# Attention plus two-layer feed-forward on one core: GpSimd's arithmetic moved to VectorE, and a new order by hand

## The chip, the core and the metric

The kernel runs on one core of a Trainium2 chip. The metric is the device time of one launch in microseconds (us). The core has five engines that run their own instruction streams and meet at semaphores: TensorE (PE in the rows; its weight loads are listed apart as PEld), VectorE (DVE), ScalarE (ACT), GpSimd (POOL) and SyncE (SP, which here only issues DMAs). Matmuls read SBUF and write PSUM; VectorE and ScalarE read both. GpSimd's queue also issues the DMAs that add to or convert what they move.

## What is computed

```python
# q, k, v: 2 x 6016 x 256; w_in: 256 x 2048; w_out: 2048 x 256; alpha: 2048
qn = q / (np.linalg.norm(q, axis=1, keepdims=True) + 1e-06)
kn = k / (np.linalg.norm(k, axis=1, keepdims=True) + 1e-06)
s = kn.transpose(0, 2, 1) @ qn / tau          # 256 x 256 for each batch
a = softmax(s)                                # over the last axis
x = (v @ a).reshape(12032, 256)
h = x @ w_in
g = np.maximum(h, 0.0) + alpha * np.minimum(h, 0.0)
return g @ w_out
```

## The kernel before

The softmax matrix of a batch is folded into the first weight: M = a @ w_in is made once for each batch, so that the first layer is one product of v and M. Every float32 operand of a matmul is split into a high part and a remainder of a shorter float type, and one product is three matmuls (`passes`: high by high, high by low, low by high).

The 12032 rows are 24 tiles of 500 to 504 (12 for each batch), and a tile is 8 **items**, one for each pair of 128-wide blocks of the 2048 hidden columns: 192 items, numbered i = 8 * tile + pair. The first layer of every item is a seven-product scheme in place of eight (`pe_a`, `pe_b`, `pe_c`, `pe_d`: 21 matmuls of 250 columns into PSUM tiles q and r). ScalarE copies q to r and p (`copies`), VectorE adds p (`add_p7`), ScalarE multiplies by alpha (`act_n`) and VectorE takes the maximum (`dve_g`), which gives g.

The second layer has two forms. In the plain form g is split (`g_high` on ScalarE, `g_low` on VectorE) and multiplied in 12 matmuls of 500 columns (`n_half`, 6 in `s2_first` and 6 in `s2_second`). In the **S form** (`is_s`) it too is a seven-product scheme, 21 matmuls of 250 columns. It needs sums of the weights, made once for each pair (`s_weights`), and sums of g (`g_sums` on VectorE, tile t), whose remainder is made by negating the high part on ScalarE (`t_low`, tile tgl) and by a DMA that adds t to it (the **adding DMA**, issued by GpSimd in `t_low`). `s2_first` holds 9 matmuls that need g alone (tiles xh, xl); `s2_second` holds the 12 that need tgh and tgl. S items are the pairs 0, 2, 4, 6 in batch 0 and 0, 1, 2, 4, 5, 6 in batch 1, in the tiles of `S_TILES`.

The sign of alpha - 1 decides between maximum and minimum; it is folded into the weights of w_out. To pay for that, h has to be multiplied by the sign. In batch 0 that is done in the maximum (a scalar_tensor_tensor with `sgn`). In batch 1 the w_in that M is made from was multiplied by it beforehand: `reload_wi` brings a part of w_in and the row of alpha back, `sign_wi` makes the sign and multiplies on GpSimd, then `split_wi_h` (ScalarE) and `split_wi_l` (VectorE) split it for `m1_pe`.

GpSimd also makes the weight sums: `s_weights` (five additions and subtractions for each of six pairs) and one subtraction in `s_weights_split`.

What sets the order: all steps from the first item on are put in one list. `put(i, at, f, ...)` gives a step the place 5.0 * i + at + MOVED, the list is sorted, and each engine runs its instructions in that order. `MOVED` is a table of shifts, one dictionary for each item of a named stretch: "first" (from item 0), "early" (which repeats for every tile), "soft" and "m1" (where the softmax and M of batch 1 are made beside the tiles of batch 0), "late" (repeats for the tiles of batch 1), "last". gh and gl (and tgh and tgl, which share their buffers) have 3 buffers each, raw (xh, xl, weight sums, w_in parts) has 4, r's first tile has 2.

Of the kernel before, what the change touches and what calls it, by code (L numbers as in the profile page):

```python
# [14 lines left out]
P = 128  # L15
# [8 lines left out]
SIDE = 3.7  # L24
# [32 lines left out]
W_ITEMS = (3, 100, 4, 6, 102, 7)  # L57
# [10 lines left out]
CHAIN = dict(sums=(2, 4.0), norms=(3, 2.0), norms2=(3, 4.0), bcast=(4, 3.7), score0=(5, 3.7),  # L68
             score1=(6, 2.0), exp0=(6, 3.7), exp1=(7, 1.7), pt=(8, 3.7), eT0=(8, 4.0), eT1=(8, 6.0))
MOVED = {  # L70
    ("first", 0): dict(add_p70=2.65, copies=-1.66, keep_wi=-4.85, pe_a=-1.98, pe_b=-1.87,
# [4 lines left out]
    ("first", 2): dict(act_n0=0.29, act_n1=0.15, add_p70=0.83, add_p71=-0.13, copies=-1.01,
        dve_g0=0.68, dve_g1=2.22, g_high0=1.69, g_high1=-0.3, g_low0=2.77, g_low1=2.8,
        pe_a=-2.34, pe_b=-2.28, pe_c=-0.67, pe_d=-2.39, pe_s2=-1.85, wo_next=0.31),
    ("first", 3): dict(act_n0=-0.49, act_n1=-0.77, add_p70=0.2, add_p71=-0.41, copies=-0.8,
# [12 lines left out]
    ("first", 6): dict(act_n0=-0.93, act_n1=0.03, add_p70=-0.17, add_p71=0.8, copies=-0.41,
        dve_g0=-0.35, dve_g1=1.1, g_high0=1.19, g_high1=0.05, g_low0=4.11, g_low1=3.63,
        pe_a=-1.39, pe_b=-0.56, pe_c=-0.53, pe_d=-1.51, pe_s2=-1.44, s_weights=5.59,
        s_weights_split=-3.34, v_low0=-1.85),
    ("first", 7): dict(act_n0=0.17, act_n1=1.1, add_p70=-0.01, add_p71=0.12, copies=0.98,
        dve_g0=0.1, dve_g1=1.34, g_high0=3.72, g_high1=0.43, g_low0=3.86, g_low1=2.9, pe_a=-3.35,
        pe_b=-0.47, pe_c=0.2, pe_d=-2.03, pe_s2=-1.18, s_weights=0.6, v_low1=-1.55, v_low2=-3.0),
    ("first", 8): dict(act_n0=-0.92, act_n1=1.3, add_p70=-0.46, add_p71=1.24, copies=-1.37,
        dve_g0=-0.32, dve_g1=0.29, evac=0.27, g_high0=-1.28, g_high1=1.67, g_low0=0.53,  # L100
        g_low1=-0.19, pe_a=-2.86, pe_b=-1.76, pe_c=-0.65, pe_d=0.4, pe_s2=-0.9,
        s_weights_split=-0.43, v_sums0=-5.6),
    ("first", 9): dict(act_n0=-1.29, act_n1=0.41, add_p70=1.14, add_p71=0.09, copies=0.95,
# [1432 lines left out]
```

## Time and profile before

| | |
|---|---|
| three timed runs | 1137.88, 1143.43 and 2400.7 us |
| their median | 1143.43 us |
| the profiled execution, its own time | 1135.38 us |
| span of its instructions | 1133.6 us |
| granted TensorE clock | 1.0 of full speed throughout |

Stages by the time in the span: 0 to 100 us products of k and q and M of batch 0; about 100 to 145 tile 0; 145 to 190 tile 1; 190 to 430 the other S tiles of batch 0; 430 to 560 the softmax of batch 1 beside tiles of batch 0; 560 to 690 M of batch 1; 690 to 1080 the S tiles of batch 1; 1080 to the end the last tile. A matmul's end is modelled in these profiles and overlaps the next one, so the idle time that PE shows is somewhat less than what a stall costs, and the idle time of PEld somewhat more.

### The profile page before, as it was taken

Reading aid. Unit: us, or ns where it says so; the run is one execution under the profiler, and the core shown is the slowest. Engines: PE = TensorE matmul, PEld = TensorE weight load, DVE = VectorE, ACT = ScalarE, POOL = GpSimd, SP = SyncE. Lnnn points to the kernel's source line nnn. Section 1 sums busy time; section 2 is a strip of 40 time slices with the busy share of each in tenths; the row PEclk is TensorE's granted clock in tenths of the full one; section 3 lists DMA queues with packets and bytes.
Section 4 is the critical chain, followed back from the end, with each engine's and each line's share of the span. In section 5 each row is a group of like instructions: output and inputs, shape, how many; then the busy total and the mean of one; then the engine's idle time right before and its main releaser. Section 6 shows DMA issues by size and latency. Waiting matters only on the chain.

```text
span 1133.6 us, 20976 instructions
## 1 busy us (share of the span) xinstructions
PE 1103.0 (97%) x7788; PEld 1028.4 (91%) x7788; DVE 971.4 (86%) x1830; ACT 911.4 (80%) x1556; POOL 193.6 (17%) x220
## 2 busy tenths in 40 slices
PE   9999999999999999999999999999999999999998
PEld 8888788999999899999988889999999999999997
DVE  6798987998898898878889878998898898898974
ACT  6798687888888888678767768888888888889874
POOL 0001521011011011011244411211211121111100
PEclk9999999999999999999999999999999999999999
DMA  9997334654654554034421216556656756656620
GB/s 333 364 324 258 93 97 104 148 126 94 147 128 108 135 122 108 19 91 90 103 68 58 70 33 133 128 107 133 134 110 123 145 109 123 133 121 124 120 55 19
DMA packets 70389, 142.81 MB, mean 126 GB/s; under 512 B 6416, under 2 KB 38416, under 8 KB 70160
## 3 DMA queue, kind: packets, MB, share of 16 engines
q0 software_dynamic: 31616, 66.22, 31.9%
q1 hardware_dynamic: 38672, 75.26, 19.5%
q8 instruction: 62, 1.02, 0.4%
q14 instruction: 39, 0.32, 0.1%
HBM read 60.83 MB, written 14.42 MB: 66 GB/s over the span
## 4 chain that ended last, share of the span: by engine, by line
PE 35%; DMA 9%; DVE 5%; ACT 4%; issue 3%; POOL 0%; ACTq 0%; POOLq 0%; DVEq 0%
DMA tgl<-t 9%; PE X L441 6%; PE X L442 6%; PE X L440 5%; PE r L440 4%; PE r L442 4%; PE r L441 4%; PE o L1214 2%; ACT g L993 2%; PE q L442 1%; PE q L441 1%; PE q L440 1%; ACT tgl L1094 1%; DVE gl L1018 1%; DVE r L980 1%
## 5 line engine op out<-in xcount | busy, mean ns | idle before, releaser
L440 PE MATMUL r<-vs,m 128*128 128x250 f32 (+1 forms) x960 | 273.8, 285 | 8.6 <-DVE r L980 7.0
L442 PE MATMUL r<-vs,m 128*128 128x250 f32 (+1 forms) x960 | 268.2, 279 | 0.0
L441 PE MATMUL r<-vs,m 128*128 128x250 f32 (+1 forms) x960 | 268.2, 279 | 0.0
L980 DVE TENSOR_TENSOR r<-r,p 128x250 f32<-128x250 f32 (+1 forms) x384 | 162.5, 423 | 62.9 <-PE r L442 50.4
L440 PEld LDWEIGHTS r<-vs,m 128*128 128x128 f32 x960 | 180.8, 188 | 22.7 <-DVE r L980 10.4
L1095 POOL DMA_DIRECT2D tgl<-t x96 | 83.2, 866 | 608.9 <-ACT tgl L1094 580.1
L441 PEld LDWEIGHTS r<-vs,m 128*128 128x128 f32 x960 | 181.1, 189 | 5.2
L993 ACT ACTIVATE g<-r,alpha_sb 128x500 f32<-128x500 f32 (+1 forms) x192 | 131.2, 686 | 63.8 <-DVE r L980 42.1
L442 PEld LDWEIGHTS r<-vs,m 128*128 128x128 f32 x960 | 181.5, 189 | 0.0
L993 ACT ACTIVATE g<-r,salpha 128x500 f32<-128x500 f32 (+1 forms) x192 | 130.2, 682 | 54.1 <-DVE r L980 29.4
L1003 DVE TENSOR_TENSOR g<-r,g 128x500 f32<-128x500 f32 (+1 forms) x192 | 128.0, 675 | 35.8 <-ACT g L993 34.3
L1005 DVE SCALAR_TENSOR_TENSOR g<-r,sgn,g 128x500 f32<-128x500 f32 (+1 forms) x192 | 140.6, 733 | 18.2 <-ACT g L993 18.0
L1018 DVE TENSOR_TENSOR gl<-g,gh 128x500 fp32r<-128x500 f32 (+1 forms) x192 | 135.5, 711 | 8.8 <-ACT gh L1014 7.6
L963 ACT COPY r<-q 128x500 f32<-128x500 f32 (+1 forms) x192 | 110.1, 573 | 32.7 <-DVE g L1005 14.0
L1014 ACT CAST gh<-g 128x500 fp32r<-128x500 f32 (+1 forms) x192 | 116.5, 615 | 21.2 <-DVE g L1005 11.5
L441 PE MATMUL X<-gl,wo 128*128 128x500 f32 (+1 forms) x320 | 125.1, 391 | 1.4 <-DVE gl L1018 1.4
L440 PE MATMUL X<-gh,wo 128*128 128x500 f32 (+1 forms) x320 | 125.3, 391 | 0.0
L442 PE MATMUL X<-gh,wo 128*128 128x500 f32 (+1 forms) x320 | 124.9, 390 | 0.0
L440 PE MATMUL q<-vs,m 128*128 128x250 f32 (+1 forms) x384 | 107.9, 281 | 0.0
L442 PE MATMUL q<-vs,m 128*128 128x250 f32 (+1 forms) x384 | 107.2, 279 | 0.0
L441 PE MATMUL q<-vs,m 128*128 128x250 f32 (+1 forms) x384 | 107.2, 279 | 0.0
L1094 ACT ACTIVATE tgl<-t 128x1000 fp32r<-128x1000 f32 (+1 forms) x96 | 99.8, 1040 | 1.8 <-DVE t L1072 1.0
(152 smaller groups left out, 2733.7 us busy)
## 6 DMA issues: line engine op xcount, KB each, us to landing
tgl<-t POOLq DMA_DIRECT2D x66, 500.0 KB, 4.6
tgl<-t POOLq DMA_DIRECT2D x30, 504.0 KB, 4.7
kqT<-kqT_dram SPq DMA_DIRECT2D x20, 512.0 KB, 3.6
kq<-k_dram SPq DMA_DIRECT2D x39, 256.0 KB, 5.4
kq<-q_dram SPq DMA_DIRECT2D x39, 256.0 KB, 5.4
v<-vT_dram SPq DMA_DIRECT2D x16, 500.0 KB, 5.4
vs<-vt POOLq DMA_DIRECT2D x32, 250.0 KB, 4.8
outT_dram<-c SPq DMA_DIRECT2D x30, 250.0 KB, 2.6
```

The costliest lines, as they stand in the source:

```text
L440: nc.tensor.matmul(out, wh, xh, start=first, stop=False, **s)
L441: nc.tensor.matmul(out, wh, xl, start=False, stop=False, **s)
L442: nc.tensor.matmul(out, wl, xh, start=False, stop=last, **s)
L963: nc.scalar.copy(r_t[i][0][:, :, :h], x[:, 0:1, :h].broadcast_to([P, 2, h]))
L980: nc.vector.tensor_tensor(out=r[1][:, n, :h], in0=r[0][:, 1, :h], in1=p7_t[i][:, :h], op=ALU.add)
L993: nc.scalar.activation(blocks(g_t[i], i, 2 * fi, 2 * fi + 2), r_t[i][fi][:, :, : half_of(i)], AF.Copy, scale=(alpha_sb if tiles[items[i][0 ...
L1003: nc.vector.tensor_tensor(out=g, in0=r_t[i][fi][:, :, : half_of(i)], in1=g, op=ALU.max)
L1005: nc.vector.scalar_tensor_tensor(out=g, in0=r_t[i][fi][:, :, : half_of(i)], scalar=sgn[:, f : f + 1], in1=g, op0=ALU.mult, op1=ALU.max,)
L1014: nc.scalar.copy(gs_t[i][0][:, fi, :w], g_t[i][:, fi * w : fi * w + w])
L1018: nc.vector.tensor_tensor(out=gs_t[i][1][:, fi, :w], in0=g_t[i][:, fi * w : fi * w + w], in1=f32(gs_t[i][0][:, fi, :w]), op=ALU.subtract,)
L1094: nc.scalar.activation(ts_t[i][1][:, :w], tt_t[i][:, :w], AF.Copy, scale=-1.0)
L1095: nc.gpsimd.dma_start(out=ts_t[i][1][:, :w], in_=tt_t[i][:, :w], accum_op=ALU.add)
```

## The change

Nothing that is computed changes, but for the place of the sign of batch 1. Six things:

1. `sign_wi` and the row of alpha are gone. `reload_wi` loads the part of w_in alone, and batch 1 uses the same scalar_tensor_tensor with `sgn` in `dve_g`, and `salpha` in `act_n`, as batch 0.
2. `s_weights` and its subtraction run on VectorE, each of the five operations as a step of its own. Their items (`W_ITEMS`) go from 3, 100, 4, 6, 102, 7 to 9, 67, 10, 11, 69, 13.
3. Tile 1 is no longer an S tile, and "early" begins one tile later.
4. Steps that held several instructions are cut in single ones that can be placed apart: `wo_next` (into `split_wo`, `conv_a`, `conv_b`), `m_sums` (into `m_scaled` and four), `m_split`, `combine`, `norms2`.
5. GpSimd keeps only memory fills at the start and DMA issues.
6. The whole of `MOVED` is new.

```diff
-W_ITEMS = (3, 100, 4, 6, 102, 7)
+W_ITEMS = (9, 67, 10, 11, 69, 13)
...
-        pe_b=0.05, pe_c=0.17, pe_d=-0.31, s2_first=-0.82, s2_second=-2.41, t_high=-2.16,
...
+        s2_first=-0.07, s2_second=-0.67, t_high=0.84, t_low=0.18, v_low0=-0.46, x_high=-0.65,
...
     def reload_wi(j):
-        x = raw.tile([P, KC + 1, 256], F32, tag="raw", name=f"wi{j}")
-        nc.sync.dma_start(out=x[:, :KC], in_=wi_kept[:, j])
-        row = alpha_row[j * 256 : j * 256 + 256]
-        nc.sync.dma_start(out=x[:, KC], in_=row.partition_broadcast(P))
-        wi_raw[j] = x
-
-    def sign_wi(j):
-        w, x = wi_raw[j][:, :KC], wi_raw[j][:, KC]
-        nc.gpsimd.tensor_scalar(out=x, in0=x, scalar1=1.0, scalar2=-2.0, op0=ALU.is_gt, op1=ALU.mult)
-        nc.gpsimd.tensor_scalar(out=x, in0=x, scalar1=1.0, scalar2=None, op0=ALU.add)
-        x = wi_raw[j][:, KC : KC + 1].broadcast_to([P, KC, 256])
-        nc.gpsimd.tensor_tensor(out=w, in0=w, in1=x, op=ALU.mult)
+        wi_raw[j] = raw.tile([P, KC, 256], F32, tag="raw", name=f"wi{j}")
+        nc.sync.dma_start(out=wi_raw[j], in_=wi_kept[:, j])
...
-            scale=(alpha_sb if tiles[items[i][0]][0] else salpha)[:, f : f + 1],
+            scale=salpha[:, f : f + 1],
...
-        if tiles[items[i][0]][0]:
-            nc.vector.tensor_tensor(out=g, in0=r_t[i][fi][:, :, : half_of(i)], in1=g, op=ALU.max)
-            return
...
-    S_TILES = [t for t in range(1, len(tiles) - 1) if t not in (per_b - 4, per_b - 1, per_b)]
+    S_TILES = [t for t in range(1, len(tiles) - 1) if t not in (1, per_b - 4, per_b - 1, per_b)]
...
+    def s_weights(n, k):
+
+        if k == 0:
+            sw_t[n] = raw.tile([P, 8, P], F32, tag="raw", name=f"sw{n}")
+        x = sw_t[n]
+        fs = slice(2 * S_J[n], 2 * S_J[n] + 2)
+        a = [f32(wo[:, l, fs]).rearrange("p f m -> p (f m)") for l in range(2)]
+        o, i0, i1, op = (
+            (x[:, 0:4].rearrange("p b m -> p (b m)"), a[0], a[1], ALU.add),
+            (x[:, 4], x[:, 1], x[:, 3], ALU.add),
+            (x[:, 5], x[:, 4], x[:, 0], ALU.subtract),
+            (x[:, 6], x[:, 1], x[:, 0], ALU.subtract),
+            (x[:, 7], x[:, 2], x[:, 5], ALU.subtract),
+        )[k]
+        nc.vector.tensor_tensor(out=o, in0=i0, in1=i1, op=op)
...
-        nc.gpsimd.tensor_tensor(out=ws[0][:, n, 1], in0=x[:, 4:8], in1=f32(ws[0][:, n, 0]), op=ALU.subtract)
+    def s_weights_low(n):
+        x = sw_t[n]
+        nc.vector.tensor_tensor(out=ws[0][:, n, 1], in0=x[:, 4:8], in1=f32(ws[0][:, n, 0]), op=ALU.subtract)
...
-            ("first", 0), ("early", NPAIR + 5), ("soft", soft + 2), ("early", soft + 2 * NPAIR),
+            ("first", 0), ("early", 2 * NPAIR + 5), ("soft", soft + 2), ("early", soft + 2 * NPAIR),
```

The two lines of `MOVED` above belong to pair 4 of a tile in "late". What they and their neighbours do to the instructions is seen in the order of each engine.

TensorE, tile 17 (batch 1), item 140 (pair 4), just ahead of the matmuls that need its adding DMA. Before:

```order
L440 MATMUL X2_17_9988<-xh140_10136,wo_114 128x250
L441 MATMUL X2_17_9988<-xl140_10137,wo_114 128x250
L442 MATMUL X2_17_9988<-xh140_10136,wo_114 128x250
L440 MATMUL r0_143_10203<-vs17_9179,m1_7_7501 128x250
L441 MATMUL r0_143_10203<-vs17_9179,m1_7_7501 128x250
L442 MATMUL r0_143_10203<-vs17_9179,m1_7_7501 128x250
L440 MATMUL X3_17_9981<-tgh140_10180,ws_1130 128x250
L441 MATMUL X3_17_9981<-tgl140_10181,ws_1130 128x250
```

And now:

```order
L486 MATMUL r0_144_10190<-vs18_9620,m1_0_6778 128x250
L487 MATMUL r0_144_10190<-vs18_9620,m1_0_6778 128x250
L488 MATMUL r0_144_10190<-vs18_9620,m1_0_6778 128x250
L486 MATMUL q145_10211<-vs18_9620,m1_1_6854 128x250
L487 MATMUL q145_10211<-vs18_9620,m1_1_6854 128x250
L488 MATMUL q145_10211<-vs18_9620,m1_1_6854 128x250
L486 MATMUL q145_10211<-vs18_9620,m1_1_6854 128x250
L487 MATMUL q145_10211<-vs18_9620,m1_1_6854 128x250
L488 MATMUL q145_10211<-vs18_9620,m1_1_6854 128x250
L486 MATMUL X3_17_9914<-tgh140_10094,ws_1472 128x250
L487 MATMUL X3_17_9914<-tgl140_10095,ws_1472 128x250
```

The matmul that reads tgl140 stood behind the first layer of item 143; it now stands behind first-layer work of items 144 and 145. From the last matmul of r of item 140 to the first that reads tgh140 or tgl140 there were 90 matmuls, and there are 120.

ScalarE, the same item, from its first multiplication by alpha to the negation that the adding DMA follows. Before:

```order
L993 ACTIVATE g140_10107<-r1_140_10025,alpha_sb_119 128x500
L700 ACTIVATE vs18_9720<-vs18_9720 128x4x250
L993 ACTIVATE g140_10107<-r0_140_10024,alpha_sb_119 128x500
L1014 CAST gh139_10093<-g139_10029 128x500
L1077 CAST xh140_10136<-g140_10107 128x750
L963 COPY r0_142_10159<-q142_10121 128x2x250
L964 COPY p7_142_10161<-q142_10121 128x250
L993 ACTIVATE g141_10164<-r1_141_10088,alpha_sb_119 128x500
L993 ACTIVATE g141_10164<-r0_141_10087,alpha_sb_119 128x500
L1094 ACTIVATE tgl140_10181<-t140_10169 128x1000
```

And now:

```order
L1045 ACTIVATE g140_10005<-r1_140_9904,salpha_111 128x500
L1154 CAST tgh138_9939<-t138_9895 128x1000
L1045 ACTIVATE g140_10005<-r0_140_9903,salpha_111 128x500
L736 ACTIVATE vs18_9620<-vs18_9620 128x4x250
L1045 ACTIVATE g141_10041<-r1_141_9981,salpha_111 128x500
L1015 COPY r0_142_10043<-q142_10028 128x2x250
L1016 COPY p7_142_10045<-q142_10028 128x250
L1131 CAST xh140_10075<-g140_10005 128x750
L1045 ACTIVATE g141_10041<-r0_141_9980,salpha_111 128x500
L1148 ACTIVATE tgl140_10095<-t140_10048 128x1000
```

The number of instructions up to the negation is the same; a cast of item 138 (tgh138) has come in and a cast of item 139 (gh139) has gone ahead of them, and the high part xh140 is cast later.

VectorE in tile 1, from the first addition to r of item 9 to the first to r of item 10 (vt2 is the sums of v for tile 2). Before:

```order
L980 TENSOR_TENSOR r1_9_1399<-r0_9_1398,p7_9_1400 128x252
L1072 TENSOR_TENSOR t8_1429<-g8_1396 128x504
L1072 TENSOR_TENSOR t8_1429<-g8_1396,t8_1429 128x252
L980 TENSOR_TENSOR r1_9_1399<-r0_9_1398,p7_9_1400 128x252
L1072 TENSOR_TENSOR t8_1429<-g8_1396,t8_1429 128x252
L1005 SCALAR_TENSOR_TENSOR g9_1454<-r1_9_1399,sgn_110,g9_1454 128x504
L980 TENSOR_TENSOR r1_10_1450<-r0_10_1449,p7_10_1451 128x252
```

And now, from the second addition to r of item 9:

```order
L1032 TENSOR_TENSOR r1_9_1373<-r0_9_1372,p7_9_1374 128x252
L1103 TENSOR_TENSOR sw2_1309<-sw2_1309 128x128
L1103 TENSOR_TENSOR sw3_1436<-wo_114 128x512
L701 TENSOR_TENSOR vt2_1364<-v2_1222,vt2_1364 128x252 x2
L1103 TENSOR_TENSOR sw2_1309<-sw2_1309 128x128
L1054 SCALAR_TENSOR_TENSOR g9_1438<-r1_9_1373,sgn_110,g9_1438 128x504
L1103 TENSOR_TENSOR sw0_1244<-sw0_1244 128x128
L1032 TENSOR_TENSOR r1_10_1419<-r0_10_1418,p7_10_1420 128x252
```

The sums t8 of the S form are gone from tile 1, and four operations of the weight sums (sw0, sw2, sw3) stand in the same place, between two additions that TensorE needs.

## Rows read from the trace of the kernel before

**Rows 1.** The page's first part: each engine's busy us, share of the span, instructions.

```profile
PE 1103.0 (97%) x7788; PEld 1028.4 (91%) x7788; DVE 971.4 (86%) x1830; ACT 911.4 (80%) x1556; POOL 193.6 (17%) x220
```

**Rows 2.** Busy time by stage: stretch, its length, then each engine's busy us (instructions).

```profile
100.00:145.00 45.00, 42.47 (x261) 37.10 (x259) 41.31 (x66) 34.93 (x68) 17.71 (x21) 1.00 0.31 102
145.00:190.00 45.00, 41.98 (x294) 38.83 (x295) 36.67 (x70) 35.83 (x64) 6.21 (x7) 1.00 0.45 110
430.00:560.00 130.00, 128.99 (x907) 119.97 (x906) 111.49 (x224) 99.49 (x179) 11.42 (x14) 1.00 0.32 75
560.00:690.00 130.00, 122.59 (x819) 110.69 (x818) 110.67 (x202) 91.78 (x173) 48.20 (x46) 1.00 0.25 66
690.00:1080.00 390.00, 381.32 (x2971) 365.07 (x2970) 344.76 (x664) 336.33 (x542) 74.35 (x84) 1.00 0.62 124
```

**Rows 3.** Waits of the whole span: engine, line, releaser: total us, times, longest us.

```profile
PEld X L441 <- DMA tgl<-t: 19.1, 33, 2.4
PE X L441 <- DMA tgl<-t: 11.9, 21, 2.2
```

**Rows 4.** Waits from 100 to 145 us, TensorE's for VectorE's remainder of g.

```profile
PEld o L1214 <- DVE gl L1018: 3.8, 4, 2.0
PE o L1214 <- DVE gl L1018: 2.5, 2, 1.7
```

**Rows 5.** Waits from 560 to 690 us, TensorE's for VectorE's addition to r.

```profile
PEld r L440 <- DVE r L980: 7.9, 8, 2.9
PE r L440 <- DVE r L980: 5.4, 5, 2.5
```

**Rows 6.** Time line of PE: start, us, engine, line, operation, tiles, columns.

```profile
442.67 0.28 PE L442 MATMUL X<-tgh,ws 128*128 128x250 f32 x1
442.79 0.28 PE L440 MATMUL X<-tgh,ws 128*128 128x250 f32 x1
...
444.90 0.39 PE L440 MATMUL X<-gh,wo 128*128 128x500 f32 x1
445.12 0.39 PE L441 MATMUL X<-gl,wo 128*128 128x500 f32 x1
```

**Rows 7.** Tile tgl: from the adding DMA's issue to its landing.

```profile
DMA to landing us min/median/max: 4.5/4.6/7.0
```

**Rows 8.** Time line of PE in tile 1: a matmul that waited for the adding DMA.

```profile
172.38 0.39 PE L441 MATMUL X<-tgl,ws 128*128 128x252 f32 x1 [2.17 <-DMA tgl<-t]
```

**Rows 9.** Time line of GpSimd and VectorE in tile 0: two remainders of g.

```profile
131.82 1.26 POOL L1048 TENSOR_TENSOR sw<-wo 128x512 f32<-128x512 f32 x1
...
130.09 4.40 DVE L1018 TENSOR_TENSOR gl<-g,gh 128x504 fp32r<-128x504 f32 x2
```

**Rows 10.** Time line of GpSimd, ScalarE, TensorE and VectorE around 585 us.

```profile
583.25 1.08 POOL L603 TENSOR_SCALAR wi<-wi 128x256 f32<-128x256 f32 x1 [10.62 <-DMA wi<-alphar_dram]
...
585.36 1.34 POOL L606 TENSOR_TENSOR wi<-wi 128x512 f32<-128x512 f32 x1
...
590.13 0.62 ACT L610 CAST wis<-wi 128x512 fp32r<-128x512 f32 x1 [3.46 <-POOL wi L606]
...
585.27 2.30 DVE L924 TENSOR_TENSOR mx<-mx 128x128 f32<-128x128 f32 x4
```

**Rows 11.** Time line of VectorE: the same four subtractions 21 us later.

```profile
606.91 1.34 DVE L924 TENSOR_TENSOR mx<-mx 128x128 f32<-128x128 f32 x4
```

**Rows 12.** VectorE's groups by line and shape, 560 to 690 us: busy, mean ns.

```profile
L1018 DVE TENSOR_TENSOR gl<-g,gh 128x500 fp32r<-128x500 f32 x18 | 13.3, 748 | 0.8 <-ACT gh L1014 0.8
```

**Rows 13.** The same, 690 to 1080 us.

```profile
L1018 DVE TENSOR_TENSOR gl<-g,gh 128x500 fp32r<-128x500 f32 x26 | 17.5, 672 | 2.0 <-ACT gh L1014 2.0
```

**Rows 14.** The whole span by line: the maximum with and without sign, another subtraction.

```profile
L1005 DVE SCALAR_TENSOR_TENSOR g<-r,sgn,g 128x500 f32<-128x500 f32 (+1 forms) x192 | 140.6, 733 | 18.2 <-ACT g L993 18.0
L1003 DVE TENSOR_TENSOR g<-r,g 128x500 f32<-128x500 f32 (+1 forms) x192 | 128.0, 675 | 35.8 <-ACT g L993 34.3
...
L614 DVE TENSOR_TENSOR wis<-wi,wis 128x512 fp32r<-128x512 f32 x8 | 5.4, 681 | 0.0
```

More of the change, by code (lines that the diff above doesn't have):

```diff
@@ new lines @@
+    ("first", 13): dict(act_n0=-1.38, act_n1=1.88, add_p70=-0.35, add_p71=-0.23, copies=-0.06,
+        dve_g0=0.09, dve_g1=1.3, g_high0=1.21, g_high1=5.18, g_low0=1.36, g_low1=3.22,
+        load_T0=-5.71, load_T1=0.38, load_T2=-0.28, pe_a=-1.22, pe_b=-2.38, pe_c=-0.58,
+        pe_d=-0.28, s2_first=-1.58, s2_second=-1.28, s_weights0=-8.01, s_weights1=-3.93,
+        s_weights2=-0.2, s_weights3=-4.13, s_weights4=1.96, s_weights_low=5.55, square_T0=-8.35,
+        square_T1=-1.31, square_T2=-3.73, v_low1=-0.18),
@@ new lines @@
+    ("first", 14): dict(act_n0=1.19, act_n1=-0.13, add_p70=1.23, add_p71=-0.24, copies=-0.44,
+        dve_g0=1.12, dve_g1=-0.23, g_high0=-0.37, g_high1=1.27, g_low0=-0.64, g_low1=3.83,
+        pe_a=-2.88, pe_b=1.28, pe_c=-2.02, pe_d=1.51, s2_first=-2.94, s2_second=-2.55,
+        s_weights_high=6.88, v_low2=-2.58),
+    ("first", 15): dict(act_n0=0.28, act_n1=1.12, add_p70=-0.85, add_p71=0.85, copies=1.64,
+        dve_g0=0.99, dve_g1=0.78, g_high0=5.63, g_high1=-0.33, g_low0=4.6, g_low1=0.78,
+        pe_a=0.02, pe_b=-0.39, pe_c=0.41, pe_d=-0.13, s2_first=1.98, s2_second=0.97,
+        s_weights_low=-0.68),
@@ new lines @@
+    ("first", 16): dict(act_n0=-1.92, add_p70=-2.3, add_p71=-0.55, copies=0.52, dve_g0=0.17,
+        dve_g1=-0.94, g_high0=0.6, g_high1=-1.57, g_low0=0.86, g_low1=-1.46, pe_a=-1.34,
+        pe_b=-1.8, pe_c=-1.23, pe_d=-1.68, s2_first=-0.34, s2_second=-1.53, v_sums0=-1.63),
+    ("first", 17): dict(act_n0=-1.45, act_n1=-1.08, add_p70=2.23, add_p71=-1.43, copies=-0.56,
+        dve_g0=-1.19, dve_g1=0.44, g_high0=3.0, g_high1=3.25, g_low0=4.69, g_low1=3.65,
+        pe_a=-1.49, pe_b=1.42, pe_c=-1.92, pe_d=-0.56, s2_first=1.84, s2_second=0.6,
+        v_high1=2.75, v_high2=3.78, v_sums1=-2.16),
@@ new lines @@
+    ("late", 7): dict(act_n0=0.29, act_n1=1.85, add_p70=0.74, add_p71=-2.26, copies=-0.16,
+        dve_g0=0.29, dve_g1=1.77, g_sums0=2.41, g_sums1=2.4, g_sums2=0.86, pe_a=-3.02,
+        pe_b=-0.05, pe_c=-2.97, pe_d=-1.09, s2_first=-2.59, s2_second=0.73, t_high=-1.68,
+        t_low=2.11, x_high=1.28, x_low=0.57),
+    ("last", 0): dict(act_n0=1.06, act_n1=2.64, add_p70=1.01, add_p71=1.41, copies=-2.62,
+        dve_g0=1.12, dve_g1=2.71, g_high0=-2.17, g_high1=1.86, g_low0=3.13, g_low1=3.33,
+        pe_a=-3.8, pe_b=-0.7, pe_c=0.39, pe_d=-0.18, pe_s2=-0.8),
@@ L333 @@
+    ("last", 6): dict(pe_s2=17.95),
 }
@@ L908, in m_pe, with m_scaled @@
                     )
-    def m_sums(at, j):
+    def m_scaled(at, j):
         b = at.b
@@ L1322, in fused_kernel @@
                 nxt += 1
-            m_sums(a0, j)
+            m_scaled(a0, j)
+            for n in range(4):
+                m_sums(a0, j, n)
             if j:
@@ L1418, in fused_kernel @@
                 put(i, TILE["copy"], combine_copy, t)
-                put(i, TILE["sums"], combine, t)
+                for n in range(3):
+                    put(i, TILE["sums"], combine, t, n)
             put(i + 1, TILE["out0"], finish_out, t, 0)
```

636 lines of the change are left out of this document (332 added, 304 removed).

## The prediction

> **What bounds it now.** I read the page's first part, then the stages, then who waited. TensorE is busy for 1103.0 of 1133.6 us and VectorE for 971.4 [rows 1]. The stage of 430 to 560 us shows what TensorE looks like when nothing is late: 128.99 of 130 us [rows 2]. So the kernel is bound by TensorE's own work, and only what TensorE waits for can be won: 30.6 us by its idle time. The loss lies in four stages [rows 2]: 2.5 us in 100 to 145, 3.0 in 145 to 190, 7.4 in 560 to 690 and 8.7 in 690 to 1080. A matmul of 250 columns follows the one before it after 0.12 us though it is shown as 0.28 long [rows 6], so each stall costs up to 0.16 us more than the idle time shows. The idle time of the weight loads counts the same stall from the load, and is my upper bound for each kind of stall; that of the matmuls is the lower.
>
> Two kinds of stall hold most of it. The first is the adding DMA: matmuls waited for tgl for 11.9 us by their own idle time (21 stalls) and 19.1 by that of the loads (33) [rows 3]. It lands 4.5 to 7.0 us after its issue [rows 7]; the worst wait, 2.17 us, is in tile 1 [rows 8], the others are spread over all S tiles, most of them under 1 us. The second is VectorE being late in the two stages where GpSimd computes: for the remainder of g in tile 0, 2.5 to 3.8 us [rows 4], and for the addition to r while M of batch 1 is made, 5.4 to 7.9 us [rows 5].
>
> **Why VectorE is late there.** Two remainders of g took 4.40 us while GpSimd computed beside them [rows 9]; at the 672 ns that one takes in batch 1 [rows 13] they would take 1.35. Four subtractions of 128 columns took 2.30 us beside GpSimd's product and 1.34 alone [rows 10, 11]. The remainder of g takes 748 ns on the mean where GpSimd computes for a third of the time, and 672 where GpSimd only issues DMAs, though it does that for 74 of 390 us [rows 2, 12, 13]. So GpSimd's arithmetic slows VectorE's operations on two SBUF tensors, and its DMA issues do not. Beside that, one stall was a plain chain: the alpha row's DMA held GpSimd for 10.62 us, GpSimd held ScalarE's cast of w_in for 3.46 [rows 10], and everything behind that cast came late.
>
> **The change, part by part.**
>
> *TensorE's work.* Tile 1 turns four S items into plain ones: 12 matmuls of 500 columns at 0.229 us for 21 of 250 at 0.117 (the start-to-start distances of [rows 6], with neighbours): 2.75 for 2.46, so 4 x 0.29 = **+1.2 us**. TensorE's order has 36 matmuls fewer, which agrees. VectorE and ScalarE lose the work of the S form there; I do not count that, since it is not what is waited for.
>
> *The adding DMA.* In the new order the matmuls that read tgl stand later. Counted over the 60 S items of batch 1, at 0.117 and 0.229 us for each matmul, the way from the last matmul of r to the first that reads tgh or tgl grows from 12.3 to 13.7 us on the mean and from 11.5 to 12.6 at the least; in batch 0 from 12.7 to 14.1. Item 140, shown above, grows from 11.9 to 15.4. On ScalarE the work from an item's alpha to the negation is about as long as before. The mean stall is 19.1 / 33 = 0.6 us by the larger count, so 1.1 to 1.4 us more should cover most; tile 1's go with its S form. The saving lies between 11.9 and 19.1, middle 15.5. Two of the six S items of a tile in batch 1 (pairs 2 and 5) get little of the new room, so I leave 1.5 us standing: **-14 us**.
>
> A rule of the Trainium skill speaks against this term: by "DMA: Bandwidth & Descriptors", section "Anatomy of one DMA", a DMA from GpSimd's queue takes about 2.0 us plus its bytes over 436 GB/s, which is 3.2 us for the 0.5 MB of tgl. An order made for that would have nothing to wait for, and the later place would bring 0. The trace has 4.5 us at the best, which is the figure that I use, and it has the stalls.
>
> *GpSimd's arithmetic gone.* TensorE's stalls on VectorE in the two stages are 2.5 + 5.4 = 7.9 us by the matmuls and 3.8 + 7.9 = 11.7 by the loads, and I take 10.5, nearer to the loads because each stall costs more than its idle time. Three quarters of it go to the change, since the work of making M stays in that stage: **-8 us**. The bounds are 0 (the stage is simply full of work: VectorE 110.7 of 130 us, [rows 2]) and -11.7.
>
> *VectorE's new work.* The sign costs 733 - 675 = 58 ns for each of 192 maxima [rows 14]: 11.1 us. A set of weight sums is one operation of 512 columns (681 ns, as the split of w_in, [rows 14]), four of 128 (1.34 us together, [rows 11]) and one more of 512: 2.7 us, six times 16 us. What hides them is VectorE's idle time, 45 us of 390 in batch 1 [rows 2] against 10 x 16 x 0.058 = 9.3 us there. It is thinnest in tiles 0 and 1, where four of the six sets, 11 us, stand between the additions that TensorE needs, as shown above (1.7 us of them in one gap). Each addition that comes late holds `pe_c` and all of TensorE behind it. Bounds: 0, and 27 if all of it came on the path. In 430 to 560 us VectorE is busy for 86% and TensorE stands for 1.0 us, which is nearer to 0; tile 1 comes to over 90%. I take **+2.5 us**, two of them in tile 1.
>
> *The rest.* The cut steps keep their operations; the alpha row's DMAs and two of the three things that M's chain waits for go, in the -8. Dropping the S form's casts in tile 1 frees ScalarE, which is not late there.
>
> Sum: 1.2 - 14 - 8 + 2.5 = -18.3, from the profiled run's own 1135.4 us to 1117.1. The three times of this kernel that lie together are 1135.4, 1137.9 and 1143.4, mean 1138.9, or 0.3% above the profiled one; the same on 1117.1 gives **1120 us** for a median.
>
> **Rivals.**
>
> *More is won.* If every stall on the adding DMA and on VectorE goes (19.1 and 11.7 us) and VectorE's new work stays hidden: 1135.4 + 1.2 - 30.8 = 1105.8, as a median 1109. For it speaks that in 430 to 560 us an order of this kind leaves TensorE 1 us of idle time in 130; against it, that landings vary from 4.5 to 7.0 us.
>
> By the Trainium skill ("Perfetto Trace Analysis", section "Identifying the Most-Contended Engine") matmul busy time flatters, and the busy share of the weight loads is the better measure; that would put 105 us up for winning instead of 30.6. In 430 to 560 us the loads are busy for 92% with TensorE never waiting, since a load is shorter than a matmul of 500 columns, so here the rule gives no more room.
>
> *The gain is eaten.* VectorE goes from 86% towards 89%, and every order is new, so what was well placed may be late: additions to r in tiles 1 and 2 and in all tiles of batch 1. At 1 us for each of the 18 S tiles that stay it costs 18 us and the time is about 1135, as a median 1138: within 2%. For it speaks that the shortest way from an item's r to its `s2_first` falls from 9.5 to 7.7 us in batch 1.
>
> *Slower.* gh and gl have three buffers, and tgh and tgl share them. In batch 1 the plain item 143 takes the buffers of item 140. In the list the cast into gh of 143 stood 3.5 after item 140's `s2_second`; it now stands 0.2 after it. ScalarE runs in order, so if tgl is late by the 2.2 us of [rows 8], the cast waits with it, and behind it the copies of q that TensorE needs next: the wait is then paid twice over. At 2.4 us (the 7.0 of [rows 7] less the median 4.6) in each of 18 S tiles it costs 43 us: 1117 + 43 = 1160, as a median 1164. It decides only if nearly every tile has such a landing; above 2% slower needs 2.3 us per tile or more. Most landings are near 4.6 us, so this is unlikely.
>
> **How the numbers follow.** The forecast (1112 to 1128 as a median) has 0.48, more won (1102 to 1112) 0.24, the gain eaten (1128 to 1145) 0.22, slower (above) 0.06. For the range I leave 2% below and a few per cent of the eaten case and the slower one above: 1104 to 1140. Two per cent of the median is 23 us, about what a measurement of this kernel can tell from no change. Against 1138.9 the line is 1116: the case of more won lies below it and a third of the forecast. Faster by over 2%: 0.40; within 2%: 0.55; slower: 0.05.
>
> **What would show it.** The adding DMA: the waits for tgl fall from 11.9 and 19.1 us to 3 and 5 or less; the landing itself stays at 4.5 to 7.0. GpSimd: its busy time falls to DMA issues alone; the remainder of g takes 672 ns in all stages; TensorE's idle time falls from 7.4 to 3 us in 560 to 690 and below 1.5 in 100 to 145. VectorE's new work: its busy time changes by less than +15 us, since the slowing that goes pays for the weight sums; a new wait of TensorE for the addition to r in 145 to 190 us of some 2 us. Wrong would be: waits for tgl as long as before (the landings moved with the order), ScalarE's cast into gh waiting for TensorE's X matmuls in every tile (the slower rival), or TensorE's waits for the addition to r growing past 10 us in batch 1 (eaten).

## The result, and the profile after

The changed kernel takes 1108.42 us (median of 1108.27 to 1108.82) against 1143.29 us for the kernel before beside it: a ratio of 0.971, 95% interval 0.968 to 0.974. On another chip it took 1108.13 us against 1137.01: 0.974 (0.973 to 0.976). So it is faster by 2.6 to 2.9%. One execution of the kernel before took 2400.7 us; it is in the median and not in the ratio. The prediction had 1120 us, within 1104 to 1140, and held "within 2%" for the likeliest; what came is the time of the rival in which more is won (1109).

The page of the kernel after, first part (as [rows 1]: busy us, share of the span, instructions), and the first line of the chain that ended last:

```profile
span 1106.8 us, 20835 instructions
...
PE 1098.9 (99%) x7752; PEld 1026.3 (93%) x7752; DVE 967.8 (87%) x1853; ACT 904.0 (82%) x1553; POOL 127.5 (12%) x156
...
PE 94%; DMA 2%; DVE 2%; ACT 1%; issue 0%; SPq 0%; ACTq 0%; DVEq 0%
```

TensorE's own busy time fell by 4 us while the span fell by 27. TensorE is now nearly all of the chain. VectorE is busy for 4 us less than in [rows 1], though it has taken over the sign and the weight sums.

The stages, kernel after, in the columns of [rows 2] (length, then PE, PEld, DVE, ACT, POOL busy, instructions in brackets):

```profile
100.00:145.00 45.00, 45.00 (x280) 40.15 (x279) 38.67 (x74) 33.88 (x66) 1.61 (x2) 1.00 0.32 103
145.00:190.00 45.00, 44.81 (x287) 40.18 (x287) 40.41 (x85) 34.00 (x67) 2.85 (x4) 1.00 0.28 80
560.00:690.00 130.00, 129.82 (x889) 119.56 (x888) 112.35 (x221) 100.41 (x185) 10.01 (x12) 1.00 0.30 72
690.00:1080.00 390.00, 390.00 (x3068) 377.05 (x3067) 355.93 (x676) 342.70 (x558) 71.94 (x82) 1.00 0.61 122
```

Against [rows 2] TensorE's idle time went from 2.5, 3.0, 7.4 and 8.7 us to 0.0, 0.2, 0.2 and 0.0. These are the four stages in which the prediction placed the loss.

Six lines from the waits of the whole span, kernel after (total us, times, longest us), and the line of tile tgl that answers to [rows 7]:

```profile
PEld r L486 <- DVE r L1032: 8.3, 30, 0.7
ACT g L1045 <- DMA tgl<-t: 7.5, 8, 2.7
ACT gh L1063 <- PE X L488: 2.6, 7, 1.6
PE r L486 <- DVE r L1032: 1.6, 5, 0.5
PEld X L487 <- DMA tgl<-t: 1.5, 2, 1.3
PE X L487 <- DMA tgl<-t: 1.1, 1, 1.1
```

```profile
DMA to landing us min/median/max: 4.5/4.6/8.2
```

The waits for the adding DMA fell from 19.1 and 11.9 us [rows 3] to 1.5 and 1.1, while the DMA itself lands no sooner than in [rows 7]. What changed is its place against TensorE's work. In the two traces the first matmul that reads tgl starts 6.0 us after the end of the negation on the mean before, and 7.1 us after it now; within 0.15 us behind the landing start 38 of 96 such matmuls before, and 4 of 92 now.

### The profile page after: what moved, and what is told of

It is laid out like the page before. It is cut to its first block, busy times and chain, and to the rows that moved or that the text cites. A ratio compares the mean times of both kernels' runs of the same rounds, so it can differ in the third digit from the quotient of the medians.

```text
span 1106.8 us, 20835 instructions
## 1 busy us (share of the span) xinstructions
PE 1098.9 (99%) x7752; PEld 1026.3 (93%) x7752; DVE 967.8 (87%) x1853; ACT 904.0 (82%) x1553; POOL 127.5 (12%) x156
## 4 chain that ended last, share of the span: by engine, by line
PE 94%; DMA 2%; DVE 2%; ACT 1%; issue 0%; SPq 0%; ACTq 0%; DVEq 0%
PE X L486 13%; PE X L487 13%; PE X L488 13%; PE r L486 11%; PE r L488 10%; PE r L487 10%; PE S L788 7%; PE o L1270 4%; PE q L488 4%; PE q L486 4%; PE q L487 4%; DMA tgl<-t 1%; PE pm L940 1%; DVE g L1054 1%; ACT g L1045 0%; DMA kqs<-q_dram 0%
## 5 line engine op out<-in xcount | busy, mean ns | idle before, releaser
L1054 DVE SCALAR_TENSOR_TENSOR g<-r,sgn,g 128x500 f32<-128x500 f32 (+1 forms) x384 | 280.4, 735 | 44.9 <-ACT g L1045 42.3
L1045 ACT ACTIVATE g<-r,salpha 128x500 f32<-128x500 f32 (+1 forms) x384 | 258.3, 681 | 58.3 <-DVE r L1032 19.9
L1149 POOL DMA_DIRECT2D tgl<-t x92 | 79.2, 861 | 572.9 <-ACT tgl L1148 422.0
L1067 DVE TENSOR_TENSOR gl<-g,gh 128x500 fp32r<-128x500 f32 (+1 forms) x200 | 133.0, 673 | 13.7 <-ACT gh L1063 13.5
L1063 ACT CAST gh<-g 128x500 fp32r<-128x500 f32 (+1 forms) x200 | 120.1, 613 | 27.7 <-DVE g L1054 24.5
L486 PE MATMUL X<-gh,wo 128*128 128x500 f32 (+1 forms) x336 | 131.6, 392 | 0.0
L487 PE MATMUL X<-gl,wo 128*128 128x500 f32 (+1 forms) x336 | 131.4, 391 | 0.0
L488 PE MATMUL X<-gh,wo 128*128 128x500 f32 (+1 forms) x336 | 131.2, 391 | 0.0
L1148 ACT ACTIVATE tgl<-t 128x1000 fp32r<-128x1000 f32 (+1 forms) x92 | 95.7, 1040 | 0.8 <-DVE t L1126 0.7
L1154 ACT CAST tgh<-t 128x1000 fp32r<-128x1000 f32 (+1 forms) x92 | 94.1, 1035 | 0.0
L1135 DVE TENSOR_TENSOR xl<-g,xh 128x750 fp32r<-128x750 f32 (+1 forms) x92 | 85.8, 932 | 0.0
```

Of the source, the lines that this page charges most:

```text
L486: nc.tensor.matmul(out, wh, xh, start=first, stop=False, **s)
L487: nc.tensor.matmul(out, wh, xl, start=False, stop=False, **s)
L488: nc.tensor.matmul(out, wl, xh, start=False, stop=last, **s)
L1045: nc.scalar.activation(blocks(g_t[i], i, 2 * fi, 2 * fi + 2), r_t[i][fi][:, :, : half_of(i)], AF.Copy, scale=salpha[:, f : f + 1],)
L1054: nc.vector.scalar_tensor_tensor(out=g, in0=r_t[i][fi][:, :, : half_of(i)], scalar=sgn[:, f : f + 1], in1=g, op0=ALU.mult, op1=ALU.max,)
L1063: nc.scalar.copy(gs_t[i][0][:, fi, :w], g_t[i][:, fi * w : fi * w + w])
```

## Experiments

Each is set beside the kernel it was made from. The kernel before had a median of 1137.01, 1136.85 and 1138.38 us in the three comparisons below, the kernel after 1108.13.

### The kernel after once more

> The changed kernel once more, as the base of the three kernels that run beside it on the same chip. Its four times lay within 0.6 us of each other, those of the kernel before between 1135 and 1143. If that spread of the kernel before comes from how late its adding DMAs land, the changed kernel, which hardly waits for them, stays at 1108 to 1109 again; if it is the chip, it spreads by several us too.

1108.13 us (1107.56 to 1108.27), ratio 0.974 (0.973 to 0.976). This is what the kernels made from the kernel after are compared with.

### What the adding DMA costs: leave it out, in both kernels

```diff
         nc.scalar.activation(ts_t[i][1][:, :w], tt_t[i][:, :w], AF.Copy, scale=-1.0)
-        nc.gpsimd.dma_start(out=ts_t[i][1][:, :w], in_=tt_t[i][:, :w], accum_op=ALU.add)
```

In the kernel before:

> The kernel before with the adding DMA left out: the remainder of the sums of g is then only the negated high part, so the output is not the reference's. No order is touched, so every matmul keeps what covers it; only the landing is gone (and its traffic, and t's buffer comes free sooner). Theory (the landing alone cost what the rows say): 12 to 19 us less, 1118 to 1125. Rival (what TensorE gains at tgl it loses at the next addition to r, as when the second parts were moved): under 8 us less, with longer waits for the addition to r.

In the kernel after:

> The changed kernel with the adding DMA left out in the same way. If its order leaves the landing the room that it needs, 0.3 to 2 us less (its waits for tgl are 1.1 and 1.5 us). If a rest of the landing is still paid somewhere else, at ScalarE's buffers for instance (it waited 7.5 us for the DMA), 4 us or more.

Before without the DMA: 1112.8 us (1112.29 to 1112.98), ratio 0.977 (0.975 to 0.979), so 25.6 us less. After without it: 1105.08 us (1104.38 to 1105.24), 3.0 us below the kernel after by the two medians, or 0.8 to 4.3 by the ratios to the kernel before. The first is more than either reading expected, the second lies between the two. The edit takes the DMA's traffic and GpSimd's issues away with the landing. The stage of the S tiles of batch 1, and the first lines on TensorE's waits for VectorE, kernel before without the adding DMA:

```profile
690.00:1080.00 390.00, 388.55 (x3060) 375.64 (x3060) 352.04 (x679) 343.22 (x558) 24.73 (x27) 1.00 0.21 49
```

```profile
PEld r L440 <- DVE r L980: 9.1, 11, 2.6
PE r L440 <- DVE r L980: 6.0, 7, 2.2
PEld o L1213 <- DVE gl L1018: 3.6, 4, 1.9
PE o L1213 <- DVE gl L1018: 2.3, 2, 1.6
```

TensorE's idle time in batch 1 falls from 8.7 to 1.5 us by the DMA alone. The waits for VectorE stay nearly as they were; in the kernel before, the remainder of g has [rows 4] and the addition to r, over the whole span:

```profile
PEld r L440 <- DVE r L980: 10.4, 13, 2.9
PE r L440 <- DVE r L980: 7.0, 9, 2.5
```

So leaving the DMA out was worth 25.6 us, more than the upper bound that the prediction took from the idle time of the loads (19.1). The time line of TensorE right behind the stall of [rows 8], kernel before (start, us), shows what the idle time leaves out:

```profile
172.61 0.28 PE L442 MATMUL X<-tgh,ws 128*128 128x252 f32 x1
172.72 0.28 PE L440 MATMUL X<-tgh,ws 128*128 128x252 f32 x1
```

The matmul that waited started at 172.38, and the next one 0.23 us later, where the next but one comes after 0.11. Each stall so costs about 0.11 us beyond its idle time. With 33 stalls that is 19.1 + 33 x 0.11 = 22.7 us, most of the 25.6. All 33 show it in the trace: the next matmul follows after 0.22 us.

The starts of the matmuls give the stalls without their modelled ends: the distance from one start to the next, less the usual one (116, 117, 227 and 229 ns for 250, 252, 500 and 504 columns), summed from 100 us on where it is over 60 ns. By these **starts** the matmuls on tgh and tgl stood for 22.0 us in the kernel before, 0.1 without the DMA and 2.4 in the kernel after. The two profiled executions differ by as much: 1135.4 and 1112.8 us.

Most of the other 3 us of the 25.6 go with TensorE's clock. The profiled execution of the kernel before was granted 1.000 of full speed, the 39 beside these experiments 0.994 to 1.000; in each of the three comparisons a clock lower by 0.001 went with a time longer by 0.8 to 1.0 us, though with much scatter. Without the DMA it was 0.998 to 1.000, in all eight executions of the kernel after 1.000. The one stretch below full speed in the trace without the DMA shows what such a fall is (2 us before it, in it and after it; the column ahead of the last two is the clock):

```profile
581.00:583.00 2.00, 0.50 (x4) 0.50 (x5) 1.62 (x4) 1.95 (x4) 0.00 (x0) 1.00 0.01 4
584.00:586.00 2.00, 2.00 (x11) 2.00 (x11) 2.00 (x4) 0.00 (x0) 0.00 (x0) 0.50 0.72 214
588.00:590.00 2.00, 2.00 (x19) 2.00 (x18) 1.83 (x4) 1.83 (x4) 0.28 (x1) 1.00 0.74 248
```

Before the fall TensorE had waited 2.18 us for VectorE's addition to r. At 0.50, the lower of the two levels (1.2 of 2.4 GHz), matmuls of 256 columns start 0.21 us apart, and 0.12 once the clock is back. From the mean clocks (0.9962 for the kernel before, 0.999 without the DMA) and the 0.95 us for each 0.001 in that comparison I estimate 2.6 us; no run has the clock alone changed.

The two kernels without the DMA also give the rest of the change: 1112.8 - 1105.1 = 7.7 us. So the 33.3 us between the kernel before and the kernel after without the DMA split into 25.6 for the landing and 7.7 for everything else, and about 3 of the landing's 25.6 come back in the kernel after (by the starts 2.1 of them at tgh and tgl, 1.2 at q and r).

### Room for the landing alone: the same twelve matmuls moved

Later in the kernel before (`s2_second` of S items):

```diff
-                put(i, o["s2"][0], s2_second, i - LAG - 1)
+                put(i, o["s2"][0] + (1.4 if is_s(i - LAG - 1) else 0.0), s2_second, i - LAG - 1)
```

> The kernel before with the matmuls that need the adding DMA put 1.4 later in the list for every S item, nothing else: from an item's last matmul of r to the first that reads tgl 13.6 us of TensorE's work on the mean in batch 1 in place of 12.3, in batch 0 13.5 in place of 12.8. Theory (TensorE came too early for the landing): the waits for tgl fall from 11.9 (matmuls) and 19.1 (loads) to below 4 and 7, and the time falls by 8 to 13 us. Rival (the landing is late because buffers and ScalarE are late, and moves along): under 4 us, with new waits of ScalarE for the gh and gl buffers.

Earlier in the kernel after:

```diff
+        ready = {x[4]: x[0] for x in plan if x[3] in (t_high, t_low)}
+        for n, x in enumerate(plan):
+            if x[3] is s2_second and is_s(x[4][0]):
+                plan[n] = (max(x[0] - 1.5, ready[x[4]] + 0.01), *x[1:])
```

> The changed kernel with the matmuls that need the adding DMA put 1.5 earlier in the list for every S item (not before their own casts): from an item's last matmul of r to the first that reads tgl it is 12.6 us of TensorE's work on the mean in batch 1 in place of 13.7, 10.5 in place of 12.6 at the least; nothing else is moved. Theory (room for the landing is what was won): waits for tgl come back, 10 us or more by the weight loads, and the time rises by 8 to 15 us to 1116 to 1124. Rival (the new order as a whole won it, the room hardly matters): under 3 us, since only TensorE's order of independent matmuls changes.

Both missed by far: 1176.27 us (ratio 1.036, 1.033 to 1.038), 39.4 us slower than before, and 1184.83 (1.041, 1.039 to 1.043), 76.7 us slower than after. Waits of the whole span, kernel before with `s2_second` later:

```profile
PEld r L440 <- DVE r L980: 42.9, 55, 2.5
PE r L440 <- DVE r L980: 30.5, 50, 2.1
PEld r L440 <- ACT r L963: 16.8, 20, 1.2
PE r L440 <- ACT r L963: 12.5, 19, 1.0
...
PEld X L441 <- DMA tgl<-t: 6.8, 14, 0.7
...
PE X L441 <- DMA tgl<-t: 3.8, 11, 0.5
```

And kernel after with `s2_second` earlier (not ahead of the casts into tgh):

```profile
PEld r L486 <- DVE r L1032: 47.9, 71, 1.6
...
PE r L486 <- DVE r L1032: 32.0, 53, 1.4
...
PEld X L486 <- ACT tgh L1154: 18.6, 15, 1.7
PE X L486 <- ACT tgh L1154: 15.6, 15, 1.5
PEld X L487 <- DMA tgl<-t: 11.8, 15, 2.1
...
PE X L487 <- DMA tgl<-t: 8.3, 9, 1.9
```

The waits for tgl moved as the theory has it: 19.1 to 6.8 in the one, 1.5 to 11.8 in the other. But in both another wait grows that is far larger: TensorE's for VectorE's addition to r and, in the first, for ScalarE's copies of q, in the second for its casts into tgh. The twelve matmuls of `s2_second` need nothing of the next item's first layer, so where they stood they gave VectorE and ScalarE the time for its q and r. Moved alone, they leave that chain bare. In neither order did the move pay by itself; in the new order the other steps moved along with it.

### GpSimd's arithmetic

The sign of batch 1 left out of the kernel before (no product with the sign, no alpha row):

```diff
-        row = alpha_row[j * 256 : j * 256 + 256]
-        nc.sync.dma_start(out=x[:, KC], in_=row.partition_broadcast(P))
...
-            put(i - 2, 2.0, sign_wi, j)
```

> The kernel before without any sign in batch 1: neither GpSimd's arithmetic on w_in nor the row of alpha nor the sign in the maximum; everything else as before. The plain maximum was worth 2.9 us in the changed kernel, and the sign in the maximum with GpSimd's part gone 3.9 us here. If these add up: 6 to 8 us less, so that GpSimd's part costs that much by itself. If the plain maximum is worth nothing in the old order, 4 us.

1131.48 us, ratio 0.995 (0.993 to 0.996): 6.9 us less, within what was expected. TensorE's busy time in 560 to 690 us goes from 122.59 [rows 2] to 125.79. That is the price of the sign on GpSimd, the alpha row's chain with it; no run has the one without the other.

The weight sums put back on GpSimd in the kernel after:

```diff
-        nc.vector.tensor_tensor(out=o, in0=i0, in1=i1, op=op)
+        nc.gpsimd.tensor_tensor(out=o, in0=i0, in1=i1, op=op)
...
-        nc.vector.tensor_tensor(out=ws[0][:, n, 1], in0=x[:, 4:8], in1=f32(ws[0][:, n, 0]), op=ALU.subtract)
+        nc.gpsimd.tensor_tensor(out=ws[0][:, n, 1], in0=x[:, 4:8], in1=f32(ws[0][:, n, 0]), op=ALU.subtract)
```

> The changed kernel with the weight sums and their last subtraction on GpSimd again, at the places that they have now; the sign stays in the maximum. Theory (GpSimd's arithmetic slows VectorE's operations on two SBUF tensors): VectorE's remainders of g and sums of v in tiles 0 to 2 and tile 8 take up to twice as long, 5 to 8 us more in all, though 16 us of sums have left VectorE; TensorE stands 1 to 4 us more, time 1109.5 to 1112.5. Rival (only the count of VectorE's work matters): VectorE is freer by 16 us and the time is the same or lower.

1110.46 us, ratio 0.976 (0.975 to 0.978): 2.3 us more than after, as expected, though VectorE's remainders of g took only 4.0 us more in all, and the sums of v nothing, where 5 to 8 were expected. The remainder of g in VectorE's groups by line and shape (busy, mean ns), first the kernel after, then with the sums on GpSimd, then the kernel before:

```profile
L1067 DVE TENSOR_TENSOR gl<-g,gh 128x500 fp32r<-128x500 f32 x124 | 82.2, 671 | 9.8 <-ACT gh L1063 9.7
L1067 DVE TENSOR_TENSOR gl<-g,gh 128x504 fp32r<-128x504 f32 x76 | 50.9, 676 | 3.9 <-ACT gh L1063 3.9
```

```profile
L1067 DVE TENSOR_TENSOR gl<-g,gh 128x504 fp32r<-128x504 f32 x76 | 54.7, 726 | 4.6 <-ACT gh L1063 4.6
```

```profile
L1018 DVE TENSOR_TENSOR gl<-g,gh 128x500 fp32r<-128x500 f32 x124 | 84.2, 682 | 6.1 <-ACT gh L1014 5.4
L1018 DVE TENSOR_TENSOR gl<-g,gh 128x504 fp32r<-128x504 f32 x68 | 51.3, 764 | 2.6 <-ACT gh L1014 2.1
```

The 128x504 shape is that of the first four tiles of each batch, and the sums were made beside such tiles in the kernel before (four sets in tile 0, two in the stage of M): 764 ns before, 676 after, 726 with the sums back on GpSimd. Two of these runs part the causes. With the sums alone off GpSimd (`b_sums_vector`, below) the shape of 504 falls from 764 to 676 and that of 500 stays (682, 681); with the sign alone off it (`b_no_sign`) that of 500 falls to 673 and that of 504 stays (764, 775).

### VectorE's new work

The sums on VectorE in the kernel before, at their old places and in one piece:

```diff
-        tt = nc.gpsimd.tensor_tensor
+        tt = nc.vector.tensor_tensor
```

> The kernel before with the weight sums on VectorE at their old places (four sets in tile 0, two in the stage of M), each set in one piece; the sign stays on GpSimd. Theory (VectorE pays 2.7 us for a set but gets back what GpSimd's arithmetic cost it): tile 0 about even, between 2 us faster and 3 us slower. Rival (a set in one piece on VectorE holds the additions that TensorE waits for): 5 us or more slower, with new waits for the addition to r in tile 0.

1140.8 us, ratio 1.004 (1.002 to 1.005): 4.0 us more, between what the theory allowed and what the rival asked. Tile 0 of this kernel:

```profile
100.00:145.00 45.00, 39.15 (x239) 33.95 (x238) 41.11 (x85) 31.80 (x61) 1.66 (x2) 1.00 0.30 101
```

TensorE falls from 42.47 [rows 2] to 39.15 there, where the kernel after has 45.00. The engine alone is no gain in the old order and in one piece. In the new order, as single operations, it gains 2.3 us (above); which of the two makes the difference was not tried.

The sign in the maximum, in the kernel before (with `reload_wi`, `sign_wi` and the scale of `act_n` as in the kernel after):

```diff
-        if tiles[items[i][0]][0]:
-            nc.vector.tensor_tensor(out=g, in0=r_t[i][fi][:, :, : half_of(i)], in1=g, op=ALU.max)
-            return
         nc.vector.scalar_tensor_tensor(
```

> The kernel before with the sign of batch 1 in the maximum: no row of alpha, no GpSimd arithmetic on w_in, everything else in the old order (the weight sums still on GpSimd). Theory (GpSimd's arithmetic and the row's DMA made VectorE and ScalarE late while M of batch 1 is made): TensorE's idle time from 560 to 690 us falls from 7.4 to 3 or 4, time lower by 4 to 7 us, and the 9 us more of VectorE's work in batch 1 are not seen. Rival (the stage is full of work anyway, and VectorE's longer maximum adds): the same time or up to 4 us more.

1133.0 us, ratio 0.997 (0.995 to 0.999): 3.9 us less, just under the 4 to 7 expected, against 6.9 where the sign is left out altogether. The same without the adding DMA:

> The kernel before with the adding DMA left out and the sign of batch 1 in the maximum. If the two parts add up, 3 to 4 us less than without the adding DMA alone; what is then left to the changed kernel's 1108 is the worth of the new table beyond the landing, with the weight sums: 5 to 12 us. If they don't add up, the two causes share stalls.

1112.52 us, ratio 0.977 (0.976 to 0.979): only 0.3 below the kernel that merely leaves the DMA out. Its two stages:

```profile
560.00:690.00 130.00, 125.93 (x849) 114.34 (x849) 113.28 (x212) 97.01 (x179) 15.97 (x17) 1.00 0.19 52
690.00:1080.00 390.00, 386.31 (x3039) 372.62 (x3038) 354.72 (x672) 340.45 (x555) 24.70 (x27) 1.00 0.21 49
```

Without the DMA TensorE's busy time in 560 to 690 us was 123.23, so the sign's move gives 2.7 us there; in 690 to 1080 it was 388.55, and 2.2 us of the gain go again. VectorE's maxima are longer there, and no landing holds TensorE beside them; that this is the cause is argued.

And the plain maximum in batch 1 of the kernel after:

```diff
         g = blocks(g_t[i], i, 2 * fi, 2 * fi + 2)
+        if tiles[items[i][0]][0]:
+            nc.vector.tensor_tensor(out=g, in0=r_t[i][fi][:, :, : half_of(i)], in1=g, op=ALU.max)
+            return
```

> The changed kernel with the plain maximum in batch 1: the multiplication by the sign is left out there, so the part of the output where alpha is above 1 would differ (alpha is below 0.3 here). VectorE has 11 us less to do, in the stage where it is fullest. Theory (the sign is hidden by VectorE's idle time): 0 to 1 us less. Rival (VectorE's queue is what still holds TensorE in batch 1): 3 us or more less.

1105.22 us (1105.05 to 1106.35), ratio 0.972 (0.970 to 0.974): 2.9 us less, almost what the rival expected. Its stage and its wait for r:

```profile
690.00:1080.00 390.00, 390.00 (x3089) 379.08 (x3088) 349.12 (x678) 345.30 (x563) 71.94 (x82) 1.00 0.61 122
```

```profile
PEld r L486 <- DVE r L1032: 6.2, 20, 0.7
```

TensorE shows no idle time here, and none in the kernel after, yet 3089 matmuls fit in the 390 us in place of 3068. A stall shorter than the 0.16 us by which a matmul is shown too long [rows 6] does not appear as idle time; the wait of the loads, 6.2 for 8.3 us, shows it, and by the starts the stalls at q and r are 10.9 us in place of 14.2. This is the fastest kernel that keeps all landings, and it serves only inputs in which alpha is below 1 everywhere, as here.

### All parts in the old order

Sign in the maximum, sums on VectorE and `s2_second` later by 1.4 (the three edits shown above), in the kernel before:

> The kernel before with all three at once: sign in the maximum, weight sums on VectorE at their old places, second parts 1.4 later; tile 1 is still an S tile and the table of shifts is the old one. Theory (the parts add up): the sum of the three alone, 12 to 20 us less than before, to 1118 to 1126. Rival (the new table, which fits all of it together, is what won): under 8 us less.

1176.23 us, ratio 1.035 (1.032 to 1.039): the same as `s2_second` later alone. The parts of the change do not add up without its order.

## Why the prediction was right, and where it was off

The range held; the forecast inside it (1112 to 1128) was missed on the low side, and the range reached down to 1104 because more won had a chance of 0.24.

**What bounds the kernel.** Right: what was won are TensorE's waits, and nearly all of it in the four stages named; TensorE is now 94% of the chain. Of the 27 us of span, 22.7 come from its idle time (30.6 before, 7.9 after) and 4 from its shown busy time, in which the refill behind a stall is counted (0.39 us for a matmul that takes 0.28 elsewhere, [rows 8]). Not all waits are gone: by the starts, stalls at r fell from 7.4 to 1.5 us in 560 to 690 us but grew from 1.0 to 5.0 in 190 to 430, mostly too short to be seen as idle time.

**The adding DMA, -14.** The mechanism was right and the size was not. By the medians the landing cost 25.6 us in the old order and costs about 3 in the new one, so the term was about -22.6; by the starts in two traces at full clock it was -19.5 (22.0 to 2.4). Two of its steps failed. The idle time of the loads was taken for an upper bound, of which the term took the middle, and it is not one: refilling after each stall adds 0.11 us. And 1.5 us were left standing for pairs 2 and 5, while loads now wait for tgl twice in all. By "DMA: Bandwidth & Descriptors" of the Trainium skill, section "Anatomy of one DMA", the later place would have brought nothing; the measured price of the landing decides against that here.

**GpSimd's arithmetic, -8.** About right: 6.9 us for the sign with the alpha row, 2.3 for the sums, 9.2 together, measured in two different orders. The remainder of g went to 671 to 676 ns in both shapes, and GpSimd's busy time to that of DMA issues, as foretold. TensorE's idle time in 560 to 690 us fell to 0.2 us, not to 3.

**VectorE's new work, +2.5.** The size came out near by luck, since the place was wrong. Tile 1 shows 0.2 us of idle time and no wait of 2 us came: the work there was placed so that it fits. What costs is the sign in batch 1, 2.9 us in the new order. The prediction had most of it hidden behind VectorE's idle time. The weight sums' own cost there was not measured, only that GpSimd is 2.3 us dearer. VectorE's busy time changed by -4 us, within "less than +15".

**TensorE's work, +1.2,** agrees with the traces: at their usual distances the matmuls of 250 to 504 columns come to 965.8 us before and 967.0 after. Tile 1 as plain tile in the old order was not tried.

**The 0.3% for the median.** This added 3 us and was wrong. The kernel after lies at 1107.6 to 1108.8, next to its profiled 1108.5. The kernel before ran from 1131.6 to 1141.3 beside the experiments, and the same kernel without the adding DMA from 1112.3 to 1113.0. The spread went with the late landings, and in part with the granted clock (above): the profiled execution, against which the 0.3% was reckoned, ran at full clock, most others of that kernel below it, and the kernel after always at full clock.

**The sum.** The rest beside the landing is -7.7 us between the two kernels without the DMA. The measured parts are -6.9, +2.9 and -2.3, and +1.2 by the prediction's own count, -5.1 together. The parts were priced in different orders (in the old one without the DMA, the move of the sign was worth 0.3 and not 4), so the 2.6 us between the two sums are no price of anything. The two traces before and after, both at full clock, add up by the starts: -19.5 us at tgh and tgl, -4.7 at gh and gl, -4.3 at q and r, +1.2 for TensorE's own work and +0.6 elsewhere are the -26.8 of the span. So the two terms for GpSimd and VectorE, forecast as -5.5 together, came to -9.1; how these 9.1 us divide between GpSimd's arithmetic gone and the new order stays open.

**The rivals.** "More is won" came, for most of its reason: by the starts the stalls at the landing and at the remainder of g went nearly whole, those at q and r from 18.5 to 14.2 us. That its number fits to a microsecond is partly luck: it counts 30.8 us of stalls where the starts give 28.6, and the 0.3% that it adds makes up for it. "Slower", by the casts into gh, is absent: ScalarE waits for TensorE's X matmuls there for 2.6 us in 7 times. "Eaten" did not come, but its mechanism is real: with the same twelve matmuls at other places it took 39 and 77 us, more than double its price of 18.

## What to carry to other kernels

Price a late DMA by leaving it out, or by the loads' idle time plus the refill behind each stall; the idle time of the matmuls alone gave less than half of what leaving it out did. A stall too short to show as idle time shows in the starts. Matmuls that depend on nothing near them are the cover of some other chain, so one does not move them for one wait without placing anew what they covered. When a kernel's times spread by 1%, look at what its engines wait for and at the clock of each execution before a profiled time is scaled: here the spread went with a transfer and, in part, with the clock.

## What was not expected of the hardware

GpSimd's arithmetic slows VectorE's operations on two SBUF tensors unevenly. In the kernel before, the remainders of g took at least 659 ns, 672 in the median and up to 3542; in the kernel after never more than 684. It is not the adding DMA: without it the mean over both shapes stayed (711 ns with it, 712 without). The subtractions of 128 columns went from 358 to 285 ns on the mean. Tile gl, kernel before and kernel after (ns min/median/max), where the second line gives the shapes of every second operation, and those subtractions, before and after:

```profile
L1018 DVE TENSOR_TENSOR gl<-g,gh x192: 659/672/3542, 105.4 to 1126.1; 128x500 fp32r<-128x500 f32 x124, 128x504 fp32r<-128x504 f32 x68
```

```profile
L1067 DVE TENSOR_TENSOR gl<-g,gh x200: 666/672/684, 103.3 to 1098.9; 128x500 fp32r<-128x500 f32 x63, 128x504 fp32r<-128x504 f32 x37
```

```profile
L924 DVE TENSOR_TENSOR mx<-mx 128x128 f32<-128x128 f32 x64 | 20.5, 358 | 1.3 <-ACT mx L917 0.7
```

```profile
L968 DVE TENSOR_TENSOR mx<-mx 128x128 f32<-128x128 f32 x64 | 16.4, 285 | 1.2 <-ACT mx L957 0.7
```

That GpSimd and VectorE contend when a VectorE operation reads two SBUF tensors is what the Trainium skill's "GPSIMD Engine Reference", section "Specifications", states; these rows agree and give a size, which the section does not.
